# VectorE's sums over the attention output, a query unit's last step and two final sums at other positions of the schedule, and the closing stores on two queues

## The chip, the core and the metric

The kernel runs on one core of one Trainium2 chip. The metric is the device time of one execution in microseconds (us); every time below is in us. The engines are named as in the profile: PE is TensorE's matmuls, PEld its weight loads, DVE is VectorE, ACT is ScalarE, POOL is GpSimd, SP is SyncE, which here issues most of the transfers.

## The reference

A layer norm feeds a cached multi-head attention and a gated feed-forward block; the two are multiplied and added to the input:

```python
xn = layernorm(x)                                  # x: 1 x 2048 x 512
q  = (xn @ wq) -> 32 heads of 128                  # wq: 512 x 4096
p  = softmax(q @ k_cache^T * 128**-0.5)            # 2048 keys a head
s  = concat_heads(p @ v_cache) @ wo                # wo: 4096 x 512
g  = silu((relu(xn @ W_gate) * (xn @ W_up)) @ W_down)   # hidden width 1792
return x + s * g
```

## The kernel before

**Blocks and positions.** The attention is cut into 128 blocks, one for each head and each quarter Q of 512 queries; block b is head b // 4, Q = b % 4. A block has eight positions, each a pair of key tiles of 128. In the main loop TensorE computes the scores of one pair (L1567, two matmuls of 512 columns), ScalarE exponentiates them (L1579), and TensorE multiplies an earlier pair by V (L1676, eight matmuls; "PV" below). The scores run three pairs ahead. After the last PV of a block VectorE takes the reciprocal of the sums (L1596) and normalises (L1599) out of the same PSUM banks into which the next block's first PV writes, so that PV waits for L1599. SP then transposes the result into OT_store (L1604).

**The ring.** Scores and all other matmuls share three PSUM slots of two banks, handed out in turn (ring_acquire). A slot comes back when its reader is done. A query unit holds a slot over several positions. In blocks marked early, position 0 computes the scores of two pairs and then the extra matmuls, so all three slots are taken at once.

**Extra work between the pairs.** A table, plan, says which extra matmuls are emitted at which (block, position); a second one, side, places work of the other engines. Each engine runs its instructions in the order of emission, so these tables set the order on every queue. The pieces that matter here:

- *Query units* (emit_unit, L1050 on TensorE, L1055 on VectorE) compute the query projections of heads 8 to 31 by a scheme with seven products for eight. A unit has steps 0 to 5; in steps 4 and 5 a second matmul accumulates into the bank which VectorE has just read, so step 5 waits for step 4's L1055. In some units VectorE writes the result to QT_sb, in others to UVR. GpSimd prepares the operands (L1015).
- *Output groups* (emit_one L1406, emit_x L1466, emit_xd L1497 and L1498): the product of the attention output with wo, for four heads at a time, again with seven products. Its operand sums run on VectorE in emit_ox: for each half c of the queries steps 0 to 2 (L1338, L1341, L1344) and a step 3 (L1347), all on SBUF tiles. A group starts 16 blocks after its heads do; blocks of a group are counted 0 to 15 from there.
- *The end.* emit_finish (L1515, L1519) and emit_base (L1528 on VectorE, L1533 on GpSimd) form the parts of the final sum that don't need the last head group. emit_final_t (L1708) adds the last group's product for the quarters Q = 0 to 2 in transposed form; its sums run in final_sum (L1752, L1756 on VectorE, or L1752 on VectorE and L1758 on GpSimd). SP turns each of the four column chunks c back with a transposing transfer (L1719, "turn" below) into FO, and a store of 512 KB (L1724) writes a quarter out. The last quarter is done by emit_final_tile (L1769) in rows, four stores of 128 KB (L1774). The kernel ends when SP has seen all stores.

Of the kernel before, what the change touches and what calls it, by code (L numbers as in the profile page):

```python
# [52 lines left out]
def bass_recurrent_scan__mha_block_cached__glu_gated_reglu__prompt_kernel(  # L53
# [19 lines left out]
    QB = S // NQ  # L73
# [43 lines left out]
    with ExitStack() as es:  # L117
# [1180 lines left out]
        def defer(n, fn):  # L1298
            later.setdefault(now[0] + n, []).append(fn)
# [400 lines left out]
        def emit_final_t(Q, c, bank):  # L1700
            if Q == 0 and c == 0:
                _wait(pe, wo_tok(gL))
            if c == 0:
                _wait_all(pe, [sem_ob[i].cur() for i in range(Q, NON, QB)])
            qs = slice(Q * NQ, (Q + 1) * NQ)
            ins = None
            for hh in range(G):
                ins = pe.matmul(ps_r[:, bank, :], Wo_sb[gL % 2][:, hh, c * 128:(c + 1) * 128],  # L1708
                                OT_store[gL % 2][:, hh, qs], start=(hh == 0), stop=(hh == G - 1))
            otok = sem_op.sig(ins)  # L1710
            ftok, mtok = final_sum(ps_r[:, bank, :], otok, gT[:, c, qs],
                                   s_acc[:, 2 * (c // 2) + Q // 2, 2 * (c % 2) + Q % 2, :],
                                   base_done[(c, Q)], Q < QB - 2)

            def turn():
                _wait(sp, ftok)
                if c == 0:
                    _wait(sp, fo_tok.get(Q - 2))
                ft_tok[Q] = sem_ft[Q].sig(sp.dma_start_transpose(FO[Q % 2][:, :, c * 128:(c + 1) * 128], gT[:, c, qs]))  # L1719

            def store():
                eng = sp if Q < QB - 2 else act
                _wait(eng, ft_tok[Q])
                fo_tok[Q] = sem_out.sig(eng.dma_start(out_t[:, 4 * Q:4 * Q + 4, :], FO[Q % 2][:]))  # L1724
# [5 lines left out]
            if c == DC - 1:  # L1730
                if Q == 0:
                    defer(6, store)
                else:
                    stores.append(store)
            return mtok

        fo_tok = {}
        ft_tok = {}
        stores = []

        def final_sum(ps, otok, gv, bv, btok, on_dve):
            _wait(dve, otok)
# [18 lines left out]
        def emit_final_tile(n, bank):  # L1761
            Q, j = divmod(n, 4)
            if j == 0:
                _wait_all(pe, [sem_ob[i].cur() for i in range(Q, NON, QB)])
                _wait(dve, sem_gn.cur())
            _wait(pe, last_ot[j // 2])
            ins = None
            for hh in range(G):
                ins = pe.matmul(ps_r[:, bank, 0:D], OT_store[gL % 2][:, hh, n * 128:(n + 1) * 128],  # L1769
                                Wo_sb[gL % 2][:, hh, :], start=(hh == 0), stop=(hh == G - 1))  # L1770
            otok = sem_op.sig(ins)
            ftok, mtok = final_sum(ps_r[:, bank, 0:D], otok, gN[:, j, :], base_n(j), base_done[n], n in (NT - 4, NT - 1))
            _wait(sp, ftok)
            sem_out.sig(sp.dma_start(out_t[:, n:n + 1, :], gN[:, j:j + 1, :]))  # L1774
            return mtok

        plan = {}
# [20 lines left out]
        for g in range(NG - 1):  # L1798
            b0 = (g + 1) * GB
            half = g < NG - 2  # L1800
            split = {} if g == 0 else {3: 6} if half else {3: 5, 8: 4}
            if g == 0:
                full, part, xs = {0: (1, 0), 12: (1, 1), 2: (7, 0), 6: (7, 1)}, (1, 3, 7, 13), {2: 4, 6: 8, 5: 10, 3: 14}
            elif half:
                full, part, xs = {0: (1, 0), 2: (1, 1), 3: (7, 0), 8: (7, 1)}, (1, 9, 12, 13), {2: 4, 6: 6, 5: 10, 3: 14}
            else:
                full, part, xs = {0: (1, 0), 2: (1, 1), 3: (7, 0), 6: (7, 1)}, (1, 7), {2: 4, 6: 8, 5: 10, 3: 12}
                at(b0 + 9, 4, (emit_one, 2, g, 4, 1, 0))
            for r, (j, q) in full.items():
# [23 lines left out]
            for c, (r, p) in enumerate(((0, 2), (3, 2)) if g else ((0, 2), (1, 2))):  # L1833
                for i in range(3):
                    side.setdefault((b0 + r, p + i), []).append((emit_ox, g, c, i))
                r, p = ((8, 5), (8, 6))[c] if half and g else ((9, 2), (9, 3))[c] if g else ((9, 2), (9, 4))[c]
                side.setdefault((b0 + r, p), []).append((emit_ox, g, c, 3))
        gu_n = [len(gu_seq)]

        def gu_items(n):  # L1840
# [42 lines left out]
                at(b, 0, o)  # L1883
        for n, (g, j, b) in enumerate(unit_at):
            first = (1, 3, 5, 6) if osteps[b][0] is emit_xd else (1, 3, 5, 6)
            second = (5, 6) if b + 1 in x_at else (3, 6) if b + 1 in early else (3, 6)
            for step, (r, p) in enumerate([(0, p) for p in first] + [(1, p) for p in second]):
                at(b + r, p, (emit_unit, 0, n, step))
            side.setdefault((b - 2, 6), []).append((prep_unit, n, 0))
            side.setdefault((b - 1, 7), []).append((prep_unit, n, 1))  # L1890
            if j in (5, 7):
                side.setdefault((b + 1, 6), []).append((add_unit, g, j))
# [11 lines left out]
            side.setdefault(sw, []).append((sum_unit_w, g))  # L1904
        fb = GB * (NG - 1)
        for i in range(4):
            side.setdefault((fb + 6 + i // 2, 4 + i % 2), []).append((emit_base, 0, i))
        for k, i in enumerate((1, 3, 0, 2)):
            side.setdefault((LB - 1, 1 + k), []).append((emit_finish, i, 0))
            side.setdefault((LB - 1, 2 + k), []).append((emit_finish, i, 1))  # L1910
        for k, (J, i) in enumerate(((3, 1), (3, 3), (1, 1), (1, 3))):
            b, p = ((LB, 1), (LB, 3), (LB, 5), (LB + 1, 0))[k]
            side.setdefault((b, p), []).append((emit_base, J, i))
            c = 2 * (J // 2) + i // 2
            b, p = ((LB, 6), (LB + 1, 1), (LB + 1, 3), (LB + 1, 5))[k]
            side.setdefault((b, p), []).append((turn_base, c))
        for k, (J, i) in enumerate(((2, 0), (2, 2), (2, 1), (2, 3), (1, 0), (1, 2), (3, 0), (3, 2))):
            b, p = ((LB + 1, 2), (LB + 1, 3), (LB + 1, 4), (LB + 2, 2), (LB + 2, 3), (LB + 2, 5), (LB + 3, 1), (LB + 3, 3))[k]
            side.setdefault((b, p), []).append((emit_base, J, i))
        side.setdefault((LB + 2, 6), []).append((sum_base,))  # L1920
        for Q in range(QB - 2):
            for c in range(DC):
                if c % 2 == 0:
                    at(LB + 2 + Q, 4 * (c // 2))
                plan[(LB + 2 + Q, 4 * (c // 2))][-1].append((emit_final_t, 1, Q, c))

        def emit_S_pair(gp):
            open_S_pair(gp)
# [114 lines left out]
```

## Time and profile before

| | before |
|---|---|
| median of 3 runs | 1244.76 us (1244.68 to 1244.88) |
| profiled execution | 1245.65 us |
| its span, first to last instruction | 1244.0 us |
| PE, DVE, ACT, POOL busy | 98%, 71%, 84%, 59% of the span |
| granted TensorE clock | 0.999 |
| DMA | 85.38 MB, mean 69 GB/s |

The profiled execution is a single one and lies 0.89 us above the median. Its rows give a start from the span's begin, a duration, the engine, the line of the kernel, the operation, what it writes and reads, and in brackets how long the engine had been idle and what ended that. SPq and ACTq are the issues of transfers on the queues of SyncE and ScalarE. Busy times of TensorE overlap from one matmul to the next, so its pace is read from the starts.

### The profile page before, as it was taken

What the parts mean: (1) busy time and instruction counts of PE and PEld (TensorE: products, weight loads), DVE (VectorE), ACT (ScalarE), POOL (GpSimd) and SP (SyncE); (2) the same over time, 40 slices, a digit from 0 to 9 for tenths busy, and PEclk for the clock granted to TensorE, in tenths of its full rate; (3) what the DMA queues carried; (4) which work ended last, traced back from release to release, by engine and by line L of the source; (5) the groups of instructions that cost most, each with busy time, mean ns of one, the idle gap of its engine ahead of it and who ended that gap; (6) DMA issues with size and microseconds to landing.
All of it is one profiled execution on the core that took longest, in us unless ns stands there. A gap on an engine that the chain in (4) does not pass through costs nothing.

```text
span 1244.0 us, 28869 instructions
## 1 busy us (share of the span) xinstructions
PE 1222.6 (98%) x11719; PEld 817.2 (66%) x11933; DVE 881.2 (71%) x1314; ACT 1039.8 (84%) x1108; POOL 732.8 (59%) x839
## 2 busy tenths in 40 slices
PE   9999999999999999999999999999999999999997
PEld 5466666776666666666666666666666666666664
DVE  7678788667676767676776777676667677675587
ACT  3457877667889998989989998989998999989994
POOL 3355876313757557655865566846765576661367
PEclk9999999999999999999999999999999999999999
DMA  9712331223222433233122322234222322238527
GB/s 275 157 31 37 80 77 23 52 48 97 54 48 52 64 70 52 48 69 61 40 35 52 73 61 52 48 69 69 48 52 59 41 52 50 50 69 143 113 35 140
DMA packets 278499, 85.38 MB, mean 69 GB/s; under 512 B 253536, under 2 KB 278368, under 8 KB 278368
## 3 DMA queue, kind: packets, MB, share of 16 engines
q1 hardware_dynamic: 277168, 82.61, 34.5%
q8 instruction: 95, 1.56, 0.6%
q10 hardware_dynamic: 1200, 0.92, 0.2%
q14 instruction: 36, 0.29, 0.1%
HBM read 36.96 MB, written 4.19 MB: 33 GB/s over the span
## 4 chain that ended last, share of the span: by engine, by line
PE 94%; issue 2%; DVE 2%; POOL 1%; ACT 1%; DMA 0%; SPq 0%; DVEq 0%; POOLq 0%
PE ps_acc L1676 36%; PE ps_r L1567 33%; PE ps_r L1050 5%; PE ps_r L1167 3%; PE ps_r L1406 3%; PE ps_r L1228 3%; PE ps_r L1466 2%; PE ps_r L914 2%; PE ps_r L733 2%; PE ps_r L729 2%; PE ps_acc L832 1%; ACT PT L1579 1%; PE ps_r L1497 1%; PE ps_r L1498 1%; DMA x_sb<-in_A_x_dram 0%
## 5 line engine op out<-in xcount | busy, mean ns | idle before, releaser
L1579 ACT ACTIVATE PT<-ps_r 128x1024 bf16<-128x1024 f32 x1024 | 989.0, 1025 | 133.0 <-PE ps_r L1567 119.6
L1676 PEld LDWEIGHTS ps_acc<-V_sb,PT 128*128 128x128 bf16 x8192 | 545.8, 98 | 229.6 <-issue 30.0
L1676 PE MATMUL ps_acc<-V_sb,PT 128*128 128x129 bf16 x8192 | 632.3, 220 | 1.7
L1567 PE MATMUL ps_r<-QT_sb,KT_sb 128*128 128x512 bf16 x1849 | 557.5, 379 | 11.4 <-DVE s_acc L1386 1.1
L1055 DVE TENSOR_TENSOR UVR<-UVR,ps_r 128x512 f32<-128x512 f32 (+1 forms) x228 | 168.7, 755 | 76.9 <-PE ps_r L1050 74.8
L1376 DVE TENSOR_TENSOR s_acc<-s_acc,ps_r 128x1024 f32<-128x1024 f32 x130 | 156.7, 1218 | 32.4 <-PE ps_r L1406 20.6
L1567 PEld LDWEIGHTS ps_r<-QT_sb,KT_sb 128*128 128x128 bf16 x2048 | 162.1, 98 | 25.6 <-DVE s_acc L1386 1.3
L1015 POOL TENSOR_TENSOR TI<-xn_sb 128x512 f16<-128x512 f16 x48 | 55.5, 1157 | 96.9 <-PE ps_r L1050 96.9
L1384 DVE TENSOR_TENSOR s_acc<-s_acc,ps_r 128x512 f32<-128x512 f32 x116 | 77.4, 685 | 22.1 <-PE ps_r L1466 18.2
L1599 DVE TENSOR_TENSOR Onorm<-ps_acc,rz_sb 128x512 bf16<-128x512 f32 x127 | 87.8, 691 | 4.4
L1596 DVE RECIPROCAL rz_sb<-ps_acc 128x4 f32<-128x4 f32 x127 | 23.1, 182 | 91.0 <-PE ps_acc L1676 90.4
L1055 DVE TENSOR_TENSOR QT_sb<-UVR,ps_r 128x512 bf16<-128x512 f32 x72 | 49.6, 688 | 51.1 <-PE ps_r L1050 48.7
L1434 POOL TENSOR_TENSOR TI<-OX 128x512 f16<-128x512 f16 x28 | 31.8, 1158 | 65.1 <-issue 65.1
L1015 POOL TENSOR_TENSOR TI<-xnT 128x512 f16<-128x512 bf16 x36 | 41.6, 1156 | 35.4 <-DVE Wq_sb L992 18.2
L1322 POOL TENSOR_TENSOR WX<-Wo_sb 128x512 f16<-128x512 bf16 x7 | 8.1, 1157 | 90.3 <-DVE Wo_sb L1312 51.1
L1015 POOL TENSOR_TENSOR TI<-xn_sb,TI 128x512 f16<-128x512 f16 x48 | 55.5, 1156 | 0.0
L1123 POOL TENSOR_TENSOR QT_sb<-UVR,UVR 128x512 bf16<-128x512 f32 x24 | 29.8, 1276 | 39.9 <-DVE UVR L1055 39.9
L1050 PE MATMUL ps_r<-TI,SI 128*128 128x512 f16 x126 | 47.8, 379 | 0.4
L1123 POOL TENSOR_TENSOR UVR<-UVR,UVR 128x512 f32<-128x512 f32 x24 | 29.8, 1273 | 29.8 <-DVE UVR L1055 29.8
L1015 POOL TENSOR_TENSOR TI<-xnT,TI 128x512 f16<-128x512 bf16 x36 | 41.7, 1157 | 0.0
L1143 POOL TENSOR_SCALAR gB<-gB 128x512 bf16<-128x512 bf16 x14 | 20.8, 1487 | 30.3 <-DVE gB L1173 30.3
L1434 POOL TENSOR_TENSOR TI<-OT_store 128x512 f16<-128x512 bf16 (+1 forms) x28 | 32.7, 1190 | 9.2 <-issue 9.2
(229 smaller groups left out, 1362.4 us busy)
## 6 DMA issues: line engine op xcount, KB each, us to landing
V_sb<-in_A_v_cache_dram SPq DMA_DIRECT2D x32, 512.0 KB, 4.3
Wq_sb<-in_A_wq_dram SPq DMA_DIRECT2D x16, 256.0 KB, 3.2
Wo_sb<-in_A_wo_dram SPq DMA_DIRECT2D x8, 512.0 KB, 4.5
out_dram<-g_sb SPq DMA_DIRECT2D x4, 512.0 KB, 4.5
OT_store<-Onorm SPq DMA_TRANSPOSE x127, 2.6
Wd_sb<-in_B_W_down_dram SPq DMA_DIRECT2D x1, 1792.0 KB, 14.4
W<-in_B_W_gate_dram SPq DMA_DIRECT2D x14, 128.0 KB, 2.4
W<-in_B_W_up_dram SPq DMA_DIRECT2D x14, 128.0 KB, 2.9
```

The costliest lines, as they stand in the source:

```text
L1015: return sem_ui.sig(pool.tensor_tensor(dst, x, y, o))
L1050: return sem_up.sig(pe.matmul(dst, lhs, rhs, start=start, stop=stop, skip_group_check=True))
L1055: dve.tensor_tensor(dst, x, ps, ALU.add))
L1123: u_tok["add"] = u_tok[("add", i)] = sem_uv.sig(pool.tensor_tensor(dst, UU[:, i, :], RR[:, i, :], ALU.add))
L1167: ins = pe.matmul(ps_r[:, bank, :], L(i), R(i), start=(i == 0), stop=(i == HC - 1))
L1376: t = sem_opa.sig(dve.tensor_tensor(dst, dst, sb, op))
L1384: t = dve.tensor_tensor(dst, dst, sb, op)
L1434: return sem_oi.sig(pool.tensor_tensor(dst, x, y, o))
L1567: ins = pe.matmul(ps_r[:, 2 * s + tt, :], KT_sb[h % 2][:, t * 128:(t + 1) * 128], QT_sb[qt_slot[(h, Q)]][:], start=True, stop=True)
L1579: act.activation(PT[pb][:], ps_r[:, 2 * s:2 * s + 2, :], ACTF.Exp, scale=scale / WSC)
L1599: dve.tensor_tensor(Onorm[ob][:], o_ap, rz_sb[:].to_broadcast([128, 4, Dh]), ALU.mult))
L1676: ins = pe.matmul(o_ap, PT[pb][:, tt, j * 128:(j + 1) * 128], V_sb[vb][:, t, 0:VW], start=(t == 0 and j % 2 == 0), stop=(t == KT - 1 and j ...
```

## The change

Positions in the tables move; nothing is computed that was not computed before. In the order on the engines:

Query units whose second block is also a block of emit_x have their last step at position 7 of that block instead of 6. TensorE, for instance in block 42 (the same piece stands 18 times); L1676 is PV, L1567 the scores, L1050 the unit's step:

```order
 L1676 MATMUL ps_acc<-V_sb,PT 128x129 x8
 L1567 MATMUL ps_r<-QT_sb,KT_sb 128x512 x2
+L1676 MATMUL ps_acc<-V_sb,PT 128x129 x8
+L1567 MATMUL ps_r<-QT_sb,KT_sb 128x512 x2
 L1050 MATMUL ps_r<-TI_128,SO_135 128x512
-L1676 MATMUL ps_acc<-V_sb,PT 128x129 x8
-L1567 MATMUL ps_r<-QT_sb,KT_sb 128x512 x2
```

The step goes behind one more pair, directly ahead of the block's last PV.

In five groups one of the two step 3 operations goes from position 6 of the group's block 8 to position 1. VectorE, end of that block; L1376 are sums of the output group, L1055 the unit's, L1596 and L1599 the block's normalisation:

```order
 L1376 TENSOR_TENSOR s_acc_116<-s_acc_116,ps_r 128x2x512 x2
+L1347 TENSOR_TENSOR OX_119<-OX_119,OT_store_117 128x2x512
 L1055 TENSOR_TENSOR QT_sb_49<-UVR_123,ps_r 128x512
 L1347 TENSOR_TENSOR OX_119<-OX_119,OT_store_117 128x2x512
 L1055 TENSOR_TENSOR QT_sb<-UVR_123,ps_r 128x512
-L1347 TENSOR_TENSOR OX_119<-OX_119,OT_store_117 128x2x512
 L1596 RECIPROCAL rz_sb_75<-ps_acc 128x4
```

One L1347 now stands ahead of both of the unit's sums, and none between the last of them and the reciprocal.

In the first group (blocks from 16 on) step 3 goes from positions 2 and 4 of block 25 to 6 and 4. VectorE in that block, with the same names:

```order
 L1376 TENSOR_TENSOR s_acc_116<-s_acc_116,ps_r 128x1024
-L1055 TENSOR_TENSOR UVR_122<-UVR_122,ps_r 128x512 x2
+L1055 TENSOR_TENSOR UVR_122<-UVR_122,ps_r 128x512 x3
+L1055 TENSOR_TENSOR UVR_122<-UVR_122,ps_r 128x1024
 L1347 TENSOR_TENSOR OX_119<-OX_119,OT_store_76 128x2x512
-L1055 TENSOR_TENSOR UVR_122<-UVR_122,ps_r 128x512
-L1055 TENSOR_TENSOR UVR_122<-UVR_122,ps_r 128x1024
+L1055 TENSOR_TENSOR UVR_122<-UVR_122,ps_r 128x512 x2
 L1347 TENSOR_TENSOR OX_119<-OX_119,OT_store_76 128x2x512
-L1055 TENSOR_TENSOR UVR_122<-UVR_122,ps_r 128x512 x2
 L1596 RECIPROCAL rz_sb_75<-ps_acc 128x4
```

The first L1347 goes behind the second pair of the unit's sums, the second one behind all of them, directly ahead of the reciprocal.

In the first group's blocks 16 and 17 the steps 0 to 2 of the first half go from positions 2, 3, 4 of block 16 to 0 and 3 of block 16 and 0 of block 17; L1338 changes places with one L1250, and L1344 goes behind block 16's normalisation. One finishing subtraction (emit_finish) and one base product (emit_base) move: the latter from ahead of block 126's final sums of position 4 to behind them.

At the end the store of quarter 1 is issued by ScalarE, behind its last copies, instead of by SP; the store of quarter 2 by SP in two halves of 256 columns instead of by ScalarE in one piece; the four row stores by ScalarE instead of SP, in the order of rows 12, 13, 15, 14. SP then issues the four turns of quarter 2 one behind the other, with no store between the third and the fourth. The diff, cut:

```diff
-            def store():
-                eng = sp if Q < QB - 2 else act
+            def store(eng=sp, lo=0, hi=DC):
                 _wait(eng, ft_tok[Q])
-                fo_tok[Q] = sem_out.sig(eng.dma_start(out_t[:, 4 * Q:4 * Q + 4, :], FO[Q % 2][:]))
+                fo_tok[Q] = sem_out.sig(eng.dma_start(out_t[:, 4 * Q:4 * Q + 4, lo * 128:hi * 128], FO[Q % 2][:, :, lo * 128:hi * 128]))
...
-            _wait(sp, ftok)
-            sem_out.sig(sp.dma_start(out_t[:, n:n + 1, :], gN[:, j:j + 1, :]))
+            def store():
+                _wait(act, ftok)
+                sem_out.sig(act.dma_start(out_t[:, n:n + 1, :], gN[:, j:j + 1, :]))
+
+            stores[n] = store
...
+            ox = ((0, 0), (0, 3), (1, 0), (1, 2), (1, 3), (1, 4), (9, 6), (9, 4))
...
-            second = (5, 6) if b + 1 in x_at else (3, 6) if b + 1 in early else (3, 6)
+            second = (5, 7) if b + 1 in x_at else (3, 6) if b + 1 in early else (3, 6)
...
         emit_M([(emit_final_t, 1, QB - 2, 2)])
-        stores.pop(0)()
         flush_last_transposes()
         emit_M([(emit_final_t, 1, QB - 2, 3)])
-        stores.pop(0)()
+        stores[1](act)
+        stores[2](sp, 0, 2)
         for n in range(NT - 4, NT, 2):
             emit_M([(emit_final_tile, 1, n), (emit_final_tile, 1, n + 1)])
+        for j in (4, 3, 1, 2):
+            stores[NT - j]()
+        stores[2](sp, 2, 4)
         sp.wait_ge(sem_out.h, sem_out.n)
```

More of the change, by code (lines that the diff above doesn't have):

```diff
@@ L1719, in turn @@
                 ft_tok[Q] = sem_ft[Q].sig(sp.dma_start_transpose(FO[Q % 2][:, :, c * 128:(c + 1) * 128], gT[:, c, qs]))
-            def store():
-                eng = sp if Q < QB - 2 else act
+            def store(eng=sp, lo=0, hi=DC):
                 _wait(eng, ft_tok[Q])
-                fo_tok[Q] = sem_out.sig(eng.dma_start(out_t[:, 4 * Q:4 * Q + 4, :], FO[Q % 2][:]))
+                fo_tok[Q] = sem_out.sig(eng.dma_start(out_t[:, 4 * Q:4 * Q + 4, lo * 128:hi * 128], FO[Q % 2][:, :, lo * 128:hi * 128]))
+            stores[Q] = store
             if Q == 0 or (Q == 1 and c < DC // 2):
@@ L1729, in emit_final_t @@
                 turn()
[L1730 to L1734, printed above, removed]
+            if c == DC - 1 and Q == 0:
+                defer(6, store)
             return mtok
@@ L1738, in bass_recurrent_scan__mha_block_cached__glu_gated_reglu__prompt_kernel @@
         ft_tok = {}
-        stores = []
+        stores = {}
         def final_sum(ps, otok, gv, bv, btok, on_dve):
@@ L1832, in bass_recurrent_scan__mha_block_cached__glu_gated_reglu__prompt_kernel @@
                 side.setdefault((b0 + r, p), []).append((prep_x, g, j, 1))
[L1833 to L1837, printed above, removed]
+            ox = ((0, 0), (0, 3), (1, 0), (1, 2), (1, 3), (1, 4), (9, 6), (9, 4))
+            if not half:
+                ox = ((0, 2), (0, 3), (0, 4), (3, 2), (3, 3), (3, 4), (9, 2), (9, 3))
+            elif g:
+                ox = ((0, 2), (0, 3), (0, 4), (3, 2), (3, 3), (3, 4), (8, 5), (8, 1))
+            for k, (r, p) in enumerate(ox):
+                side.setdefault((b0 + r, p), []).append((emit_ox, g, *((k // 3, k % 3) if k < 6 else (k - 6, 3))))
         gu_n = [len(gu_seq)]
@@ L1906, in bass_recurrent_scan__mha_block_cached__glu_gated_reglu__prompt_kernel @@
         for i in range(4):
[L1907 to L1910, printed above, removed]
+            side.setdefault((fb + ((6, 4), (6, 5), (7, 4), (7, 5))[i][0], ((6, 4), (6, 5), (7, 4), (7, 5))[i][1]), []).append((emit_base, 0, i))
+        for i, part, (r, p) in ((1, 0, (11, 1)), (1, 1, (11, 2)), (3, 0, (11, 2)), (3, 1, (11, 3)), (0, 0, (11, 2)), (0, 1, (11, 4)), (2, 0, (11, 4)), (2, 1, (11, 5))):
+            side.setdefault((fb + r, p), []).append((emit_finish, i, part))
         for k, (J, i) in enumerate(((3, 1), (3, 3), (1, 1), (1, 3))):
-            b, p = ((LB, 1), (LB, 3), (LB, 5), (LB + 1, 0))[k]
-            side.setdefault((b, p), []).append((emit_base, J, i))
+            b, p = ((0, 1), (0, 3), (0, 5), (1, 0))[k]
+            side.setdefault((LB + b, p), []).append((emit_base, J, i))
             c = 2 * (J // 2) + i // 2
@@ L1917, in bass_recurrent_scan__mha_block_cached__glu_gated_reglu__prompt_kernel @@
         for k, (J, i) in enumerate(((2, 0), (2, 2), (2, 1), (2, 3), (1, 0), (1, 2), (3, 0), (3, 2))):
-            b, p = ((LB + 1, 2), (LB + 1, 3), (LB + 1, 4), (LB + 2, 2), (LB + 2, 3), (LB + 2, 5), (LB + 3, 1), (LB + 3, 3))[k]
-            side.setdefault((b, p), []).append((emit_base, J, i))
+            b, p = ((1, 2), (1, 3), (1, 4), (2, 4), (2, 3), (2, 5), (3, 1), (3, 3))[k]
+            side.setdefault((LB + b, p), []).append((emit_base, J, i))
         side.setdefault((LB + 2, 6), []).append((sum_base,))
[L1921 to L1925, printed above, removed]
+        for (Q, c), (b, p) in (((0, 0), (2, 0)), ((0, 2), (2, 4)), ((1, 0), (3, 0)), ((1, 2), (3, 4))):
+            at(LB + b, p, (emit_final_t, 1, Q, c), (emit_final_t, 1, Q, c + 1))
         def emit_S_pair(gp):
```

## The prediction

> **What bounds the kernel now.** I read the page first, then TensorE's waits, then timelines of the places that the change touches. In the page stand the span, the busy time and the chain of work that ended last:
>
> ```profile
> span 1244.0 us, 28869 instructions
> PE 1222.6 (98%) x11719; PEld 817.2 (66%) x11933; DVE 881.2 (71%) x1314; ACT 1039.8 (84%) x1108; POOL 732.8 (59%) x839
> PE 94%; issue 2%; DVE 2%; POOL 1%; ACT 1%; DMA 0%; SPq 0%; DVEq 0%; POOLq 0%
> ```
>
> TensorE (PE) sets the time almost to the end; a drain of some 10 us follows (from 1233.59 in part 5's rows), through VectorE (DVE), GpSimd (POOL) and the stores. No arithmetic is added or removed. So the change pays only where TensorE stands still because VectorE is late, and in the drain. The waits of TensorE's weight loads (engine, line, releaser: us in total, times, longest) show one kind that the change addresses:
>
> ```profile
> PEld ps_r L1050 <- DVE UVR L1055: 4.3, 11, 0.4
> PEld ps_r L1050 <- DVE QT_sb L1055: 3.2, 7, 0.5
> ```
>
> These 18 are the last step of 18 query units. The sum of 7.5 us overstates the price: a weight load runs ahead of its matmul, so most of such a wait costs the matmuls nothing. I price every place by matmul starts. Between them TensorE's own pace is 0.43 for a pair of score matmuls (four take 0.86), 0.45 for a pair's eight PV matmuls, 0.22 for one 512-wide matmul: rows below (510.55 to 512.30 is PV 0.45, scores 0.86, two matmuls 0.43).
>
> **Part 1: last unit step from position 6 to 7, 18 places.** One of them, before (start, duration, instruction):
>
> ```profile
> 508.94 0.59 PE L1567 MATMUL ps_r<-QT_sb,KT_sb 128*128 128x512 bf16 x2
> ...
> 509.44 0.39 PE L1050 MATMUL ps_r<-TI,SO 128*128 128x512 f16 x1
> ...
> 509.86 0.69 DVE L1055 TENSOR_TENSOR UVR<-UVR,ps_r 128x512 f32<-128x512 f32 x1 [0.48 <-PE ps_r L1050]
> ...
> 510.55 0.62 PE L1676 MATMUL ps_acc<-V_sb,PT 128*128 128x129 bf16 x8
> ...
> 511.20 0.18 DVE L1596 RECIPROCAL rz_sb<-ps_acc 128x4 f32<-128x4 f32 x1 [0.65 <-PE ps_acc L1676]
> ...
> 512.30 0.62 PE L1676 MATMUL ps_acc<-V_sb,PT 128*128 128x129 bf16 x8
> ```
>
> Removed: the step's matmul should start at 508.94 + 0.43 = 509.37 and starts at 509.44, so 0.07 is lost, 18 x 0.07 = 1.3 us. Added: at position 7 the same step stands just ahead of the block's reciprocal on VectorE. Call its matmul's start T. The add starts at T + 0.42 and lasts 0.69, so VectorE is free at T + 1.11 at the latest. The last PV group starts at T + 0.22, and the reciprocal, 0.65 later in the row, wanted to start at T + 0.87. The next block's first PV matmul follows a late reciprocal by 1.04 (part 2's rows: 494.01 to 495.05), so at T + 2.15; TensorE alone would be there at T + 0.22 + 1.75 = T + 1.97. That loses up to 0.18. VectorE starts an independent operation some 0.08 before the one ahead is recorded as done (part 3's rows: 361.18 + 1.93 = 363.11, next at 363.03), which makes it 0.10. The ring slot of the unit is freed later too (T + 1.11, wanted by the second score pair at T + 1.10), inside the same delay. Net 0.10 - 0.07 = +0.03 to +0.11 a place; I take +0.04, 18 x 0.04 = **+0.7**. Bounds: -1.3 (the reciprocal's delay stays hidden) to +2.0. GpSimd's next operands, which wait for this matmul, start about 0.9 later; they are needed a block later, which hides it.
>
> **Part 2: L1347 from block position 6 to 1, five groups.** Block 8 of a group, before:
>
> ```profile
> 490.15 0.68 DVE L1347 TENSOR_TENSOR OX<-OX,OT_store 128x1024 f16<-128x1024 f16 x1
> ...
> 493.02 1.07 DVE L1347 TENSOR_TENSOR OX<-OX,OT_store 128x1024 f16<-128x1024 f16 x1
> ...
> 494.01 0.17 DVE L1596 RECIPROCAL rz_sb<-ps_acc 128x4 f32<-128x4 f32 x1
> ...
> 494.34 0.59 PE L1406 MATMUL ps_r<-OT_store,WX 128*128 128x512 bf16 x2
> ...
> 495.05 0.61 PE L1676 MATMUL ps_acc<-V_sb,PT 128*128 128x129 bf16 x8
> ...
> 901.17 0.72 DVE L1347 TENSOR_TENSOR OX<-OX,OT_store 128x1024 f16<-128x1024 f16 x1
> ```
>
> The second L1347 stands ahead of the reciprocal, and PV starts at 495.05 instead of 494.34 + 0.43 = 494.77: 0.28 lost. At position 1 the operation has its operands (they wait for a matmul of block 7) and lies after two sums, with nothing due on VectorE until the unit step of position 3. Five places of 0.28 would be 1.4; in one of the five the operation takes 0.72 instead of 1.07 (the row at 901.17), so I take **-1.3**. Bounds: -1.4, and -0.7 if ScalarE, 84% busy, takes half of it back.
>
> **Part 3: L1347 in block 25, from positions 2 and 4 to 4 and 6.**
>
> ```profile
> 360.56 0.38 PE L1050 MATMUL ps_r<-TI,SI 128*128 128x512 f16 x1
> ...
> 361.18 1.93 DVE L1055 TENSOR_TENSOR UVR<-UVR,ps_r 128x512 f32<-128x512 f32 x2
> ...
> 363.01 1.16 POOL L1015 TENSOR_TENSOR TI<-xn_sb 128x512 f16<-128x512 f16 x1 [1.47 <-PE ps_r L1050]
> 363.03 1.69 DVE L1347 TENSOR_TENSOR OX<-OX,OT_store 128x1024 f16<-128x1024 f16 x1
> ...
> 363.65 0.38 PE L1050 MATMUL ps_r<-xn_sb,SO 128*128 128x512 f16 x1
> ...
> 364.75 0.62 PE L1676 MATMUL ps_acc<-V_sb,PT 128*128 128x129 bf16 x8
> ...
> 365.97 1.04 PE L1567 MATMUL ps_r<-QT_sb,KT_sb 128*128 128x512 bf16 x4 [0.60 <-DVE UVR L1055]
> ```
>
> The scores should follow at 364.75 + 0.45 = 365.20 and come at 365.97: 0.77 lost, waiting for the unit's sums behind the L1347 of 1.69. That one started 0.02 after a GpSimd instruction and ended 0.55 after that instruction's end (364.17); alone it takes 0.68 (row 490.15). With the earlier L1347 gone from position 2, the pair of sums starts 0.42 after its matmul (360.98, not 361.18), and the L1347 at 362.83, now 0.18 ahead of GpSimd. If it then takes 0.68, the last sum waits only for its matmul (363.65 + 0.42 + 0.69 = 364.76), and the stall goes. The other L1347, now behind that sum, ends near 365.5, about when the reciprocal is due (364.75 + 0.65 = 365.40). **-0.8**; bounds -0.8 to +0.6 (rival 1). The Trainium skill ("SBUF — State Buffer", "Who interferes with whom") says that a VectorE operation with two SBUF inputs and a reading GpSimd one exclude each other, and that whichever issues first goes through whole. By that rule the 0.18 decides everything, for -0.8; the trace agrees with 0.68, 1.07 and 1.69 for one shape.
>
> **Part 4: block 16 and the finishing sums.** L1344 leaves its place ahead of the reciprocal:
>
> ```profile
> 282.98 1.59 DVE L1344 TENSOR_TENSOR OX<-OT_store 128x1024 f16<-128x1024 f16 x1
> ...
> 284.87 0.59 PE L1406 MATMUL ps_r<-OT_store,WX 128*128 128x512 bf16 x2
> ...
> 285.53 1.07 PE L1676 MATMUL ps_acc<-V_sb,PT 128*128 128x129 bf16 x16
> ```
>
> PV starts 285.53 - 284.87 - 0.43 = 0.23 late, which goes. But L1338 ahead of it changes places with another VectorE operation beside a busy GpSimd and may end up to 0.2 later: **-0.1** (-0.3 to +0.2). The one swapped finishing subtraction in block 123 stays in the same run of VectorE work: 0.
>
> **Part 5: block 126 and the drain.** A base product moves behind the final sums of position 4:
>
> ```profile
> 1214.77 3.05 DVE L1528 SCALAR_TENSOR_TENSOR s_acc<-s_acc,gT 128x512 f32<-128x512 f32 x2
> ...
> 1217.75 0.69 DVE L1752 SCALAR_TENSOR_TENSOR ps_r<-ps_r,gT 128x512 f32<-128x512 f32 x1
> ...
> 1220.54 0.11 PEld L1567 LDWEIGHTS ps_r<-QT_sb,KT_sb 128*128 128x128 bf16 x2 [0.31 <-DVE gT L1756]
> ```
>
> With one product ahead the final sum starts about 0.4 earlier and the 0.31 wait goes: -0.3. Both products then stand ahead of the reciprocal, filling the room that is won. In the drain, by queue:
>
> ```profile
> 1233.59 0.65 ACT L1653 COPY OT_store<-ps_r 128x256 bf16<-128x256 bf16 x2 [0.57 <-PE ps_r L1648]
> ...
> 1236.73 0.58 SPq L1724 DMA_DIRECT2D out_dram<-FO  x1
> ...
> 1237.36 1.60 SPq L1719 DMA_TRANSPOSE FO<-gT  x1
> ...
> 1240.82 0.39 ACTq L1724 DMA_DIRECT2D out_dram<-FO  x1
> ```
>
> ```profile
> out_dram<-FO ACTq DMA_DIRECT2D x1, 512.0 KB, 3.2
> FO<-gT SPq DMA_TRANSPOSE x12, 2.5
> ```
>
> The end is store Q=2: 1240.82 + 3.2 = 1244.0. It waits for the last turn, which SP issues at 1237.36, behind store Q=1. After the change that store goes out on ACT after 1234.24, and the turn follows the one before it at about 1236.7, 0.66 earlier; it lands 2.5 later if alone (3.46 in this row, beside the store). Then 256 KB go out, and 256 KB more 0.58 behind. The earliest: 1236.4 + 2.5 + 0.58 + 2.6 (an estimate for half of 512 KB) = 1242.1; the latest keeps 3.46 and 3.2 behind the 0.58: 1236.7 + 3.46 + 0.58 + 3.2 = 1243.9. I take 1242.9, a little on the early side, since store Q=1 starts over 2 earlier and is mostly through before the last turn; so **-1.1** for part 5 with its -0.3 (-1.9 to -0.1). SP's final wait and the four row stores, now on ACT, are ready before. The Trainium skill ("SBUF — State Buffer", "The DMA setup-cost knee") speaks against halves: each transfer pays some 2 us whatever its size, so coalesce. By its figures a whole is an estimated 3.2 (the row's value) and a half 2.6, so the pair ends no earlier than one store; the gain would be only the earlier turn.
>
> **The sum.** +0.7 - 1.3 - 0.8 - 0.1 - 1.1 = -2.6. The profiled execution took 1245.65 around its span of 1244.0, and would take 1243.05. It lies 0.89 above the median of 1244.76; the median becomes 1242.16, called **1242.2**. About 0.2% (2.5 us) is what a measurement of this kernel can tell from no change, so the forecast lies just beyond that bound.
>
> **Rivals.**
> 1. GpSimd wins block 25. If L1347 starts just behind GpSimd's instruction, the 0.77 stays, and the second L1347 delays the reciprocal by about 0.5: +0.6 instead of -0.8, 1243.6. For it: the margin is 0.18; against: both starts hang on matmuls of the same row.
> 2. The stores give nothing. Store Q=1 now shares the DMA engines with the turns of Q=2, the last turn lands as late as before, and the halves add an issue. Part 5 shrinks to -0.3: 1243.0.
> 3. Slower: the moved step costs what L1347 did. If the add at position 7 delays PV by 0.35 net at all 18 places, as a late 1.07 did with 0.28, part 1 is +6.3, not +0.7: 1247.8. It ends above the start from 0.18 net a place ((2.6 + 0.7) / 18). For it: the place ahead of the reciprocal is the tightest of a block; against: 0.69 is shorter, and the slack sums to 0.1.
> 4. The move does what it says: the wait goes and the reciprocal's delay stays hidden, part 1 is -1.3: 1240.2.
>
> **How the numbers follow.** Forecast 0.58 (its own range -4.0 to -1.4, 1240.8 to 1243.4; beyond 0.2% in 0.36 of it, within in 0.22), rival 4 0.13, rival 1 0.11, rival 2 0.09, rival 3 0.09. Faster 0.36 + 0.13 = 0.49; same 0.22 + 0.11 + 0.09 = 0.42; slower 0.09. The range goes from 1240.4, the lower end of the forecast with the upper part of rival 4, to 1244.1, past rivals 1 and 2 with some lost savings; it leaves out rival 3 and more than half of rival 4, some 0.17, and the far ends of the others.
>
> **What would show it.** The 18 waits of L1050 for L1055 are gone, and PV after such a block starts about 0.1 after TensorE's own pace. PV after block 8 follows L1406 by 0.43. In block 25 L1347 starts before GpSimd's instruction and takes 0.7, with no stall of the scores. The last turn follows the one before it without a gap, and the last store lands within 6.5 of its issue. I am wrong if ScalarE's wait for scores shrinks while PV's wait for it grows, or if the drain from TensorE's last matmul to the end keeps its length.

## The result, and the profile after

The changed kernel takes 1241.46 us (median of 9 runs, 1241.14 to 1241.58) against 1244.80 (9 runs, 1244.65 to 1244.88): 3.34 us less, ratio 0.9973, 95% interval 0.9963 to 0.9983. Forecast were 1242.2, between 1240.4 and 1244.1. The total is inside the range, but not all of its terms are right: the forecast gain of block 16 was too small by 1.08 and that of block 25 too large by 0.8, each more than the 0.74 by which the total was off.

The page of the profiled execution (its own time 1241.50):

```profile
span 1239.9 us, 29084 instructions
PE 1232.4 (99%) x11933; PEld 817.3 (66%) x11933; DVE 876.3 (71%) x1314; ACT 1039.6 (84%) x1108; POOL 729.8 (59%) x839
PE 96%; POOL 1%; DVE 1%; issue 1%; DMA 0%; ACT 0%; POOLq 0%; DVEq 0%
```

The span fell by 4.1, the median by 3.34. That difference is itself a finding (block 25, below). VectorE's (DVE) share of the chain fell from 2% to 1%. TensorE's 98% and 99% aren't to be compared: the trace of before holds 11719 matmul records for 11933 weight loads, so 214 are missing there. The waits of TensorE's weight loads, before and then after (engine, line, releaser: us in total, times, longest):

```profile
PEld ps_r L1567 <- DVE s_acc L1386: 1.3, 1, 1.3
PEld ps_r L1567 <- DVE UVR L1055: 0.8, 1, 0.8
```

```profile
PEld ps_r L1567 <- DVE UVR L1055: 4.3, 11, 0.4
PEld ps_r L1567 <- DVE QT_sb L1055: 3.2, 7, 0.5
PEld ps_r L1567 <- DVE s_acc L1386: 0.3, 1, 0.3
```

The 18 waits of L1050 for L1055 have not gone: the same 4.3 and 3.2 us stand now at the scores, L1567. The single waits of before for L1386 (1.3, block 16) and for the unit's sums (0.8, block 25) have shrunk or gone.

To see where the time went I took the start of each block's reciprocal (L1596) in both timelines and followed by how much it lies earlier. A step is counted when the following blocks keep it. Up to rounding the sum is the span's, which goes from 1244.01 to 1239.88:

| place | forecast | between the two traces |
|---|---|---|
| start of the program, before any edit | 0 | +0.09 |
| block 16 | -0.1 | -1.18 |
| blocks 25 to 27 | -0.8 | -0.78 |
| 18 unit steps | +0.7 | 0.0 |
| five groups, block 8 of each | -1.3 | -1.24 |
| block 123, finishing subtractions | 0 | -0.24 |
| block 126, base product | -0.3 | -0.31 |
| drain, from ScalarE's last copies (L1653) to the end | -0.8 | -0.46 |
| sum | -2.6 | -4.13 |

### The profile page after: what moved, and what is told of

The parts are those of the page before. It is cut to its first block, busy times and chain, and to the rows that moved or that the text cites. A ratio compares the mean times of both kernels' runs of the same rounds, so it can differ in the third digit from the quotient of the medians.

```text
span 1239.9 us, 29084 instructions
## 1 busy us (share of the span) xinstructions
PE 1232.4 (99%) x11933; PEld 817.3 (66%) x11933; DVE 876.3 (71%) x1314; ACT 1039.6 (84%) x1108; POOL 729.8 (59%) x839
## 4 chain that ended last, share of the span: by engine, by line
PE 96%; POOL 1%; DVE 1%; issue 1%; DMA 0%; ACT 0%; POOLq 0%; DVEq 0%
PE ps_acc L1676 37%; PE ps_r L1567 35%; PE ps_r L1050 5%; PE ps_r L1167 3%; PE ps_r L1406 3%; PE ps_r L1228 3%; PE ps_r L1466 2%; PE ps_r L914 2%; PE ps_r L729 2%; PE ps_r L733 2%; PE ps_acc L832 1%; PE ps_r L1497 1%; PE ps_r L1498 0%; POOL gT L1755 0%; POOL s_acc L1533 0%
## 5 line engine op out<-in xcount | busy, mean ns | idle before, releaser
L1676 PEld LDWEIGHTS ps_acc<-V_sb,PT 128*128 128x128 bf16 x8192 | 545.1, 98 | 231.1 <-issue 29.6
L1676 PE MATMUL ps_acc<-V_sb,PT 128*128 128x129 bf16 x8192 | 632.2, 220 | 0.0
L1567 PE MATMUL ps_r<-QT_sb,KT_sb 128*128 128x512 bf16 x2048 | 605.1, 379 | 0.2 <-DVE s_acc L1386 0.2
L1055 DVE TENSOR_TENSOR UVR<-UVR,ps_r 128x512 f32<-128x512 f32 (+1 forms) x228 | 168.7, 756 | 85.2 <-PE ps_r L1050 83.0
L1376 DVE TENSOR_TENSOR s_acc<-s_acc,ps_r 128x1024 f32<-128x1024 f32 x130 | 156.8, 1219 | 32.6 <-PE ps_r L1406 22.5
L1567 PEld LDWEIGHTS ps_r<-QT_sb,KT_sb 128*128 128x128 bf16 x2048 | 161.2, 98 | 26.4 <-DVE UVR L1055 4.3
L1599 DVE TENSOR_TENSOR Onorm<-ps_acc,rz_sb 128x512 bf16<-128x512 f32 x127 | 87.8, 692 | 4.4
L1055 DVE TENSOR_TENSOR QT_sb<-UVR,ps_r 128x512 bf16<-128x512 f32 x72 | 49.5, 688 | 52.8 <-PE ps_r L1050 50.4
L1596 DVE RECIPROCAL rz_sb<-ps_acc 128x4 f32<-128x4 f32 x127 | 23.1, 182 | 82.7 <-PE ps_acc L1676 82.1
L1434 POOL TENSOR_TENSOR TI<-OX 128x512 f16<-128x512 f16 x28 | 31.8, 1156 | 65.1 <-issue 65.1
L1050 PE MATMUL ps_r<-TI,SI 128*128 128x512 f16 x126 | 47.8, 379 | 0.0
L1434 POOL TENSOR_TENSOR TI<-OT_store 128x512 f16<-128x512 bf16 (+1 forms) x28 | 32.1, 1170 | 8.7 <-issue 8.0
```

Of the source, the lines that this page charges most:

```text
L1050: return sem_up.sig(pe.matmul(dst, lhs, rhs, start=start, stop=stop, skip_group_check=True))
L1055: dve.tensor_tensor(dst, x, ps, ALU.add))
L1376: t = sem_opa.sig(dve.tensor_tensor(dst, dst, sb, op))
L1434: return sem_oi.sig(pool.tensor_tensor(dst, x, y, o))
L1567: ins = pe.matmul(ps_r[:, 2 * s + tt, :], KT_sb[h % 2][:, t * 128:(t + 1) * 128], QT_sb[qt_slot[(h, Q)]][:], start=True, stop=True)
L1599: dve.tensor_tensor(Onorm[ob][:], o_ap, rz_sb[:].to_broadcast([128, 4, Dh]), ALU.mult))
```

## The experiments

Medians and ranges in us; "beside" is the median of the runs of before taken with them. The diffs below are cut to the entries that differ.

| run | median (range) | beside | ratio (95%) |
|---|---|---|---|
| p1_step7 | 1245.02 (1244.59 to 1246.19) | 1245.50 | 0.9996 (0.9988 to 1.0005) |
| p2_sum81 | 1243.95 (1243.47 to 1244.77) | 1245.50 | 0.9988 (0.9979 to 0.9997) |
| p34_first | 1243.59 (1243.47 to 1243.92) | 1245.50 | 0.9985 (0.9976 to 0.9994) |
| p5_end | 1244.59 (1243.64 to 1244.96) | 1245.50 | 0.9993 (0.9984 to 1.0002) |
| b25_only | 1244.85 (1244.67 to 1246.21) | 1245.47 | 0.9997 (0.9988 to 1.0006) |
| b16_swap | 1243.75 (1243.66 to 1244.96) | 1245.47 | 0.9989 (0.9981 to 0.9998) |
| b16_late | 1245.25 (1244.36 to 1245.89) | 1245.47 | 0.9998 (0.9989 to 1.0006) |
| a_46 | 1243.17 (1242.69 to 1243.49) | 1245.47 | 0.9983 (0.9974 to 0.9992) |
| a_whole | 1241.21 (1240.85 to 1241.29) | 1244.81 | 0.9971 (0.9960 to 0.9982) |
| a_early | 1241.28 (1240.85 to 1241.73) | 1244.81 | 0.9971 (0.9961 to 0.9982) |
| a_56 | 1241.64 (1241.25 to 1242.16) | 1244.81 | 0.9975 (0.9965 to 0.9984) |
| a_early_act | 1241.12 (1240.84 to 1241.42) | 1244.79 | 0.9971 (0.9960 to 0.9982) |

Before itself does not repeat to 0.2 us. Of the 33 runs beside the first four kernels, 8 lie at 1244.63 to 1244.98 and 25 at 1245.35 to 1246.15; of the next 33, 14 lie at or below 1245.05 and 19 at or above 1245.42. Of the 17 beside a_whole, a_early and a_56, 15 lie at or below 1245.14, and of the 11 beside a_early_act, 10 at or below 1244.92. So where fractions of a us are told of below, they come from the traces, place by place, and from a kernel's lower group.

**p1_step7**: the moved unit step alone.

```diff
-second = (5, 6) if b + 1 in x_at
+second = (5, 7) if b + 1 in x_at
```

> The kernel before with the query unit's last step at position 7 instead of 6 in the 18 places, and nothing else. Reading of the two traces: the wait of 0.39 to 0.46 us of a weight load moves from L1050 to the second score pair of the next position, whose ring slot the unit frees, and costs the matmuls 0.07 there as it did before; no change, 0.0 +- 0.3 us, with 18 waits of L1567 for L1055 in the trace. The prediction: +0.7 us. Its rivals: -1.3 us (the wait vanishes), +6.3 us (the reciprocal is delayed 0.35 at each place).

From block 27 to block 126 no reciprocal stays displaced (-0.91 at both). Seven of the 11 runs lie at 1244.59 to 1245.15, the other four at 1245.54 to 1246.19; the lower group of before is 1244.63 to 1244.98. The move gives nothing and costs nothing. This also held the surprise of the study: block 25, whose order here is that of before, lost its stop.

**p2_sum81**: L1347 of five groups from (8, 6) to (8, 1).

```diff
-((8, 5), (8, 6))[c] if half and g
+((8, 5), (8, 1))[c] if half and g
```

> The kernel before with L1347 of five groups at position 1 of block 8 instead of 6, and nothing else. Reading of the two traces: 0.24 to 0.25 us at each of five reciprocals, -1.24 us, PV 0.43 behind L1406. The prediction: -1.3 us, with -0.7 us if ScalarE takes half of it back. Rival: the gain was the unit's step being moved out of the way in the same blocks, then under -0.5 us.

The five lowest runs lie at 1243.47 to 1243.64, so about -1.2, and the trace gives -1.19 over the five groups. In this kernel the unit's steps stand where they stood, so the rival falls.

**p34_first**: only the first group's table.

```diff
+ox = ((0, 0), (0, 3), (1, 0), (1, 2), (1, 3), (1, 4), (9, 6), (9, 4))
```

> The kernel before with only the first group's sums at their new places (blocks 16, 17 and 25). Reading of the two traces: -1.2 us at block 16 and -0.8 us at blocks 25 to 27, -2.0 us in all. The prediction: -0.1 and -0.8, -0.9 us. Rival for the size: the stop of 1.11 us at block 16 is particular to the one profiled execution of before, which lies 0.9 us above its median; then the median falls by about 1.1 us though the trace shows 2.

The trace gives -1.24 at block 16's reciprocal, of which -1.18 is left at the next, and -0.78 at blocks 25 to 27. But the median lies only 1.2 below the lower group of before, with all 11 runs within 0.45: the rival's form, except that the stop that is not in every execution is that of block 25, not that of block 16.

**p5_end**: only the changes from block 123 on, with the unit step and the sums as before.

> The kernel before with only the changes from block 123 on: order of the finishing subtractions, the base product, the stores and their queues. Reading of the two traces: -0.25 us at block 123 (pairs of dependent subtractions are taken apart), -0.31 at block 126, -0.43 in the drain, -1.0 us in all. The prediction: 0, -0.3 and -0.8, -1.1 us. Rival: the stores give nothing, -0.55 us.

The trace repeats all three pieces: -0.24 at block 123, -0.31 at block 126, -0.45 in the drain. The times (1243.64, 1244.01, then nine from 1244.49 to 1244.96) are before's two groups moved by about that.

**b25_only**: of the first group only one L1347 moves.

```diff
-(9, 2), (9, 4)
+(9, 6), (9, 4)
```

> The kernel before with only the first L1347 of block 25 moved from position 2 to 6. Theory now: in before L1347 and GpSimd's L1015 start within 0.02 us of each other there, and which of them goes first is settled anew in each execution; 0.8 us hangs on it, and the runs of before lie in two heaps, about 1244.8 and 1245.6. Here L1347 is 0.17 ahead, so every run belongs to the lower heap: 1244.6 to 1245.0, spread under 0.5 us, and against before 0 to -0.8 us after how many of its runs lie in the upper heap. The prediction: -0.8 us in every run. Rival: the heaps have another cause (clock, transfers), and this kernel's runs show them too.

Ten of 11 runs lie at 1244.67 to 1245.12, and one, unexplained, at 1246.21. What decides block 25 is seen by holding p1_step7, whose order there is that of before, against the changed kernel (start, duration, instruction):

```profile
362.88 1.71 POOL L1015 TENSOR_TENSOR TI<-xn_sb 128x512 f16<-128x512 f16 x1 [1.48 <-PE ps_r L1050]
362.89 0.69 DVE L1347 TENSOR_TENSOR OX<-OX,OT_store 128x1024 f16<-128x1024 f16 x1
```

```profile
361.75 0.69 DVE L1347 TENSOR_TENSOR OX<-OX,OT_store 128x1024 f16<-128x1024 f16 x1
361.92 1.53 POOL L1015 TENSOR_TENSOR TI<-xn_sb 128x512 f16<-128x512 f16 x1 [1.81 <-PE ps_r L1050]
```

In the profiled execution of before the two started 0.02 apart, GpSimd (POOL) took 1.16 and L1347 took 1.69. In p1_step7 they start 0.01 apart, L1347 takes 0.69 and GpSimd 1.71. The same order of instructions thus ends either way. All five kernels that keep before's order there (p1_step7, p2_sum81, p5_end, b16_swap, b16_late) drew the second outcome in their profiled executions, whose own times all lie in the lower group of their kernels; before's profile, at 1245.65, drew the first. In the changed kernel VectorE is 0.17 ahead, and its 9 runs lie within 0.44. So the -0.78 is real against the profiled execution and absent against the 9 runs of before in the result, all of which lie in the lower group. Without it the traces give -4.13 + 0.78 = -3.35; measured are -3.34. That the lower runs of before itself lack the stop is inferred, since only one execution of before was profiled, and it lies in the upper group.

**b16_swap** and **b16_late** take block 16 apart: only L1338 ahead of L1250, and only L1344 behind the normalisation.

```diff
-(0, 2), (0, 3), (0, 4)
+(0, 0), (0, 3), (0, 4)     # b16_swap
+(0, 2), (0, 3), (1, 0)     # b16_late
```

> The kernel before with only L1338 of block 16 ahead of the L1250 instead of behind it. Theory: GpSimd's L1434 waits for that L1250, so it now starts behind VectorE's L1341, which takes 0.68 instead of 1.53, and the copies L1386 that TensorE waits 1.11 us for start about 0.9 earlier: -0.9 us, seen at block 16. Rival: the gain of block 16 comes from L1344, which stays here: 0 to -0.1 us. The prediction had +0.2 us for the exchange as its upper end.

> The kernel before with only L1344 of the first half moved behind the normalisation of block 16; L1250 and L1338 stay as they were. Theory: only the 0.23 by which PV was late goes, -0.2 us, and TensorE still stops 1.1 us for the copies L1386. Rival: it is L1344 that gave block 16's 1.2 us: -1.2 us.

At block 16's reciprocal b16_swap gains 1.07 and b16_late 0.27 (0.21 at the next block's). The first timeline is b16_swap, the second b16_late:

```profile
278.92 0.68 DVE L1341 TENSOR_TENSOR OT_store<-OT_store 128x1024 f16<-128x1024 bf16 x1
...
282.04 0.11 PEld L1567 LDWEIGHTS ps_r<-QT_sb,KT_sb 128*128 128x128 bf16 x2 [0.33 <-DVE s_acc L1386]
```

```profile
278.99 1.53 DVE L1341 TENSOR_TENSOR OT_store<-OT_store 128x1024 f16<-128x1024 bf16 x1
...
282.96 0.11 PEld L1567 LDWEIGHTS ps_r<-QT_sb,KT_sb 128*128 128x128 bf16 x2 [1.29 <-DVE s_acc L1386]
```

The exchange alone shortens L1341 from 1.53 to 0.68 and TensorE's wait from 1.29 to 0.33. Moving L1344 alone leaves both.

**a_46**: the changed kernel with the unit's last two steps at positions 4 and 6, **a_56** with them at 5 and 6 as in before.

```diff
-second = (5, 7) if b + 1 in x_at
+second = (4, 6) if b + 1 in x_at     # a_46
+second = (5, 6) if b + 1 in x_at     # a_56
```

> The changed kernel with the query unit's last two steps at positions 4 and 6 instead of 5 and 7 in the 18 places: step 5 then has a whole pair between it and the sum that it waits for. Theory: the 0.07 lost at each place (0.13 where the sum goes to QT_sb) goes, -1.3 to -1.6 us. Rival: the ring slot is held one position longer with only two left for the scores, a pair of 0.88 us is then shorter than ScalarE's 0.95 for an exponential, and 0.1 us a place comes back: about 0 us. Prediction's rival 3 in another place: over 0.2 us a place, slower by 3 us or more.

> The changed kernel with the query unit's last step back at position 6, so that the 18 places are as in before and all the rest is changed. Theory (the wait only moved from L1050 to L1567): 0.0 +- 0.2 us. The prediction: -0.7 us (the move costs 0.04 a place). Rival 4 of the prediction: +1.3 us.

a_46 is a miss: its median is 1.7 above that of the changed kernel, its span 1.5. The rival named the right shortage, a slot held while only two are left, but it priced it too low and expected the wait at the scores. A place in a_46, and the wait summed over the kernel:

```profile
505.01 0.59 PE L1567 MATMUL ps_r<-QT_sb,KT_sb 128*128 128x512 bf16 x2
...
505.62 0.10 PEld L1050 LDWEIGHTS ps_r<-TI,SI 128*128 128x128 f16 x1 [0.51 <-ACT PT L1579]
```

```profile
PEld ps_r L1050 <- ACT PT L1579: 9.1, 18, 0.5
```

The unit's step 4, one position earlier, finds no free slot: its weight load and its matmul start at 505.62 instead of 505.01 + 0.43 = 505.44, behind ScalarE's exponential (ACT), and lose 0.18 where step 5 had lost 0.07. This wait stands at all 18 places. In a_56 the wait is back at L1050, and the span is that of the changed kernel, 1239.9; the medians differ by 0.18 with overlapping ranges. The forecast cost of the move (0.7) isn't there.

**a_whole**, **a_early** and **a_early_act**: the store of quarter 2 in one piece; its first half behind a semaphore of its own, so that it waits only for its two turns; and that half issued by ScalarE.

```diff
-stores[2](sp, 0, 2)
+stores[2](sp)               # a_whole, without the second half
-ft_tok[Q] = sem_ft[Q].sig(...)
+P = Q + (Q == QB - 2 and c >= 2)
+ft_tok[P] = sem_ft[P].sig(...)   # a_early, a_early_act
```

> The changed kernel with the store of quarter 2 in one piece of 512 KB on SP's queue instead of two halves. In its trace the halves are issued at 1236.16 and 1236.59 and the end is 1239.9. Theory from the rows of before (512 KB in 3.2 us when alone): 1236.16 + 3.2 = 1239.4, -0.4 to -0.5 us, so the halves cost. Rival: the store is limited by its bytes next to the row stores, 3.6 to 3.9 us: 0 to +0.2 us.

> The changed kernel with the first half of quarter 2's store waiting for its own two turns alone (a semaphore of its own), not for all four. SP then issues it right behind the last turn, about 1235.0 instead of 1236.16, and only the second half behind the last turn's landing. Theory: the end comes at 1236.2 plus 2.6 to 3.1 for 256 KB, -0.6 to -1.1 us. Rival: the last turn, in flight beside that half, lands later (3.46 beside a store in before, against 2.5), which gives back most of it: -0.2 to 0 us.

> The variant with the early first half of quarter 2's store, that half now issued by ScalarE instead of SP, so about 1233.1 (when its two turns have landed) instead of 1234.9. Theory (the end is set by the bytes still to move: the DMA engines are full from 1236.5 to 1239.0 and 0.59 busy from 1235 to 1236): 256 KB at about 300 KB/us leave that stretch, -0.5 to -0.8 us against the early half on SP (1241.28). Rival: the last turn is issued by SP beside this store and takes 1.8 to 1.9 us instead of 1.3 to issue, as the second turn did beside the store of quarter 1, so the second half starts 0.6 later: 0 to +0.2 us.

All three end 0.2 to 0.3 us below the changed kernel, and their ranges overlap with its range and with one another, so only the sign is likely. In a_whole SP's last wait is no longer for this store but for a row store (issue of the store, then the wait):

```profile
1236.03 0.38 SPq L1723 DMA_DIRECT2D out_dram<-FO  x1
```

```profile
SPq L2014 <- DMA out_dram<-gN: 3.0, 1, 3.0
```

In a_early the last turn, beside the early half, lands 2.61 after its issue (2.48 in the changed kernel), and the last transfer to land is again a row store. In a_early_act the half leaves earlier still, and the last turn pays (turn, ScalarE's half, SP's half):

```profile
1233.57 1.26 SPq L1720 DMA_TRANSPOSE FO<-gT  x1
1236.83 0.39 SPq L1724 DMA_DIRECT2D out_dram<-FO  x1
```

```profile
1234.36 0.39 ACTq L1724 DMA_DIRECT2D out_dram<-FO  x1
```

The turn's issue stays at 1.26, so the rival's mechanism falls; but SP's half, which waits for that turn, comes 3.26 behind its issue instead of 1236.16 - 1233.67 = 2.49 in the changed kernel. The gain of the earlier half is mostly given back there. a_early_act has the lowest median of all, 1241.12, but its range overlaps those of a_whole and a_early.

## Why the prediction was right or wrong, point by point

**Part 1 (+0.7 forecast, 0.0 found): the mechanism was right, its place and size were not.** A place in the changed kernel:

```profile
508.15 0.38 PE L1050 MATMUL ps_r<-TI,SO 128*128 128x512 f16 x1
...
508.82 1.10 PE L1567 MATMUL ps_r<-QT_sb,KT_sb 128*128 128x512 bf16 x4
...
509.17 0.17 DVE L1596 RECIPROCAL rz_sb<-ps_acc 128x4 f32<-128x4 f32 x1
509.31 0.11 PEld L1567 LDWEIGHTS ps_r<-QT_sb,KT_sb 128*128 128x128 bf16 x2 [0.39 <-DVE UVR L1055]
...
510.22 0.61 PE L1676 MATMUL ps_acc<-V_sb,PT 128*128 128x129 bf16 x8
```

With T = 508.15 the reciprocal comes at T + 1.02 and PV at T + 2.07, the forecast delay of 0.10 to the hundredth. Most of it, 0.07, falls already on the scores (four take 1.10 instead of 1.03), which wait for the ring slot; I had named that wait and counted it inside. It is as large as the 0.07 that went at L1050, and the remaining 0.03 is gone again by the next block's reciprocal, so the net is 0.0. Rival 4 falls since the wait did not go, rival 3 since 0.35 a place is nowhere.

**Part 2 (-1.3 forecast, -1.24 found)** came nearly as worked out, with 0.24 to 0.25 at each of the five places, also at the one that was counted for less (the row at 901.17). The operation at its new place, then the reciprocal and PV:

```profile
486.56 0.70 DVE L1347 TENSOR_TENSOR OX<-OX,OT_store 128x1024 f16<-128x1024 f16 x1
...
491.81 0.18 DVE L1596 RECIPROCAL rz_sb<-ps_acc 128x4 f32<-128x4 f32 x1 [0.58 <-PE ps_acc L1676]
...
492.47 0.59 PE L1406 MATMUL ps_r<-OT_store,WX 128*128 128x512 bf16 x2
...
492.90 0.62 PE L1676 MATMUL ps_acc<-V_sb,PT 128*128 128x129 bf16 x8
```

PV follows L1406 by 0.43, which is TensorE's own pace.

**Part 3 (-0.8 forecast): right in the trace, wrong in the sum.** VectorE came 0.17 ahead (0.18 forecast), took 0.69, and the stop went. The step that failed is the one from the profiled execution to the median: I took that one execution as typical and subtracted only its 0.89 as an offset. That 0.89 over the median held this very stop, so against the median the term was to be 0. The row carried the warning, two starts 0.02 apart. The rule that I cited from the Trainium skill ("SBUF — State Buffer", "Who interferes with whom"), that the first to issue goes through whole, agrees with the changed kernel (VectorE 0.17 ahead: 0.69 beside 1.53) and with the profile of before (GpSimd 0.02 ahead: 1.16 beside 1.69). In p1_step7 GpSimd's recorded start is 0.01 ahead and VectorE still goes through whole (0.69 beside 1.71). So at 0.01 to 0.02 the recorded starts don't tell the winner, which differs between these two executions of the same order. Rival 1 falls, since VectorE keeps its lead in the changed kernel.

**Part 4 (-0.1 and 0 forecast, -1.18 and -0.24 found): two terms mis-sized.** In block 16 I asked only how long L1338 would take after the exchange, up to 0.2 more. I did not ask who waits for L1250. Before, then after (L1338 stands ahead of L1250):

```profile
276.83 0.71 DVE L1250 SCALAR_TENSOR_TENSOR g_sb<-dbuf,dbuf 128x512 bf16<-128x512 f32 x1
...
277.46 1.64 DVE L1338 TENSOR_TENSOR OX<-OT_store 128x1024 f16<-128x1024 bf16 x1
...
278.52 1.60 POOL L1434 TENSOR_TENSOR TI<-OT_store 128x512 f16<-128x512 bf16 x1
...
279.14 1.53 DVE L1341 TENSOR_TENSOR OT_store<-OT_store 128x1024 f16<-128x1024 bf16 x1
...
280.59 2.47 DVE L1386 COPY s_acc<-ps_r 128x512 f32<-128x512 f32 x4
...
283.11 0.61 PE L1567 MATMUL ps_r<-QT_sb,KT_sb 128*128 128x512 bf16 x2 [1.11 <-DVE s_acc L1386]
```

```profile
276.92 0.70 DVE L1338 TENSOR_TENSOR OX<-OT_store 128x1024 f16<-128x1024 bf16 x1
277.55 1.64 DVE L1250 SCALAR_TENSOR_TENSOR g_sb<-dbuf,dbuf 128x512 bf16<-128x512 f32 x1
...
279.11 0.68 DVE L1341 TENSOR_TENSOR OT_store<-OT_store 128x1024 f16<-128x1024 bf16 x1
279.36 1.45 POOL L1434 TENSOR_TENSOR TI<-OT_store 128x512 f16<-128x512 bf16 x1 [0.72 <-DVE g_sb L1250]
...
279.71 2.47 DVE L1386 COPY s_acc<-ps_r 128x512 f32<-128x512 f32 x4
...
282.24 0.61 PE L1567 MATMUL ps_r<-QT_sb,KT_sb 128*128 128x512 bf16 x2 [0.15 <-DVE s_acc L1386]
```

GpSimd's preparation (prep_x, L1434) waits for the L1250 that was emitted ahead of it (sem_dg.cur()). With L1250 behind L1338, GpSimd stands idle for 0.72 and starts behind L1341, which then needn't wait for it. The copies L1386 start 0.88 earlier, and TensorE's stop of 1.11 shrinks to 0.15. VectorE gained nothing from the exchange itself, since the second of its two operations takes 1.64 in either order; the gain came because GpSimd was held back. b16_swap shows it alone.

In block 123 I called the swapped subtraction free, since it "stays in the same run of VectorE work". Before:

```profile
1190.42 0.80 DVE L1519 TENSOR_TENSOR s_acc<-s_acc 128x512 f32<-128x512 f32 x1
1191.14 0.68 DVE L1515 TENSOR_TENSOR s_acc<-s_acc 128x512 f32<-128x512 f32 x1
...
1191.86 0.69 DVE L1519 TENSOR_TENSOR s_acc<-s_acc 128x512 f32<-128x512 f32 x1
...
1192.46 0.68 DVE L1515 TENSOR_TENSOR s_acc<-s_acc 128x512 f32<-128x512 f32 x1
```

L1519 reads what the L1515 ahead of it wrote, and in the kernel waits for that one's semaphore: it starts 0.72 after it (1191.14 to 1191.86). The next, independent L1515 follows after 0.60. (The first L1519, 0.80 long, runs beside GpSimd.) After:

```profile
1188.03 1.28 DVE L1515 TENSOR_TENSOR s_acc<-s_acc 128x512 f32<-128x512 f32 x2
1189.23 1.28 DVE L1519 TENSOR_TENSOR s_acc<-s_acc 128x512 f32<-128x512 f32 x2
```

Here two pairs are interleaved, with starts 0.60 apart, which saves 2 x 0.12 = 0.24, and these sums stand ahead of the reciprocal that PV waits for. p5_end repeats the 0.24; no run undid the order by itself.

**Part 5 (-1.1 forecast, -0.77 found).** The -0.3 of block 126 came as -0.31. The drain's step that failed is the earlier turn: "0.66 earlier" became nothing. The second turn before, then ScalarE's last copies and SP's transfers after (ACTq is ScalarE's issue):

```profile
1234.12 1.26 SPq L1719 DMA_TRANSPOSE FO<-gT  x1
```

```profile
1229.92 0.37 ACT L1653 COPY OT_store<-ps_r 128x256 bf16<-128x256 bf16 x1 [0.63 <-PE ps_r L1648]
1230.04 0.40 ACTq L1723 DMA_DIRECT2D out_dram<-FO  x1
```

```profile
1230.39 1.93 SPq L1719 DMA_TRANSPOSE FO<-gT  x1
1232.36 1.27 SPq L1719 DMA_TRANSPOSE FO<-gT  x1
1233.67 1.29 SPq L1719 DMA_TRANSPOSE FO<-gT  x1
1236.16 0.38 SPq L1723 DMA_DIRECT2D out_dram<-FO  x1
1236.59 0.57 SPq L1723 DMA_DIRECT2D out_dram<-FO  x1
```

Everything ahead of the drain is 3.67 earlier (ScalarE's copies: 1233.59, now 1229.92), and 1237.36 - 3.67 = 1233.69: the last turn is issued when it was. The second turn, just behind ScalarE's store, takes 1.93 to issue instead of 1.26, and that uses up what SP saved by not issuing the store. The gain is only that the last turn lands after 2.49 instead of 3.46, against 0.5 that the halves take longer (1236.16 to 1239.9 is 3.7, the whole store of before 3.2). That agrees with the Trainium skill's advice against halves ("SBUF — State Buffer", "The DMA setup-cost knee") as far as a_whole's 0.25 goes, whose range overlaps. Rival 2 falls, since the last turn lands sooner and the drain is 0.46 shorter. Why the second turn's issue is longer behind ScalarE's store stays open; no run moved that store alone.

So the forecast came near by luck: Part 3 (0.8 too much gain) and Part 5 (0.3 too much) stood against Parts 1 and 4 (2.0 too little between them). The two signs of being wrong did not appear: PV's waits for ScalarE stayed at 2.9 in all, and from ScalarE's last copies to the end the drain went from 10.42 to 9.96.

## What to carry to other kernels

Before a saving read from one profiled execution is subtracted from a median, look whether that execution holds a stop that hangs on two starts a few hundredths of a us apart; if it lies above the median by about that stop, the saving isn't in the median. When two operations change places, ask for each who waits for it: here the gain came from holding GpSimd back, whose work had been in VectorE's way. And the wait for a unit's sum didn't go when its step was moved by a pair, it went to whoever wanted the ring slot next.

## What the runs showed of the hardware that I had not expected

- A VectorE and a GpSimd operation that slow each other here (0.69 beside 1.71, 1.69 beside 1.16) and start 0.01 to 0.02 us apart came out in either order in the profiled executions, with the same order of instructions; the times of before fall into two groups some 0.8 us apart. Which group is drawn differed from series to series (low were 9 of 9, 8 of 33, 14 of 33, 15 of 17, 10 of 11); what decides it stays open.
- On VectorE an operation of 0.69 on SBUF starts 0.72 after the one whose result it reads and waits for, but 0.60 after one that it doesn't depend on.
- In the drains of before and after, a transposing transfer takes 1.19 to 1.29 us to issue on SP's queue, 1.60 right behind a 512 KB store on the same queue, and 1.93 just behind one on ScalarE's queue. Beside a store in flight the last turn lands 3.26 (a_early_act) and 3.46 (before) after its issue, not 2.49.
